# A gated mix of a long convolution and a two-layer network: the first loads in another order, and the front's constants set anew

## The chip, the cores and the metric

One core of a Trainium2 chip runs the whole program. The metric is the time of one execution in microseconds (us), told by the device. PE is the matrix engine (PEld its loads of the stationary operand), DVE the vector engine, ACT the scalar engine with its function tables, POOL the general engine, and SP the engine that issues most DMAs.

## The reference, cut to what matters

```python
g = sigmoid((x * gate_w).sum(-1, keepdims=True))           # x: 1 x 2048 x 512
a = conv_s4(x, ...)                                        # K[d, l] from exp(dt * A * l), FFT convolution, + x * Dskip
b = gelu(x @ w1 + b1) @ w2 + b2                            # 512 -> 1792 -> 512, gelu by tanh
return g * a + (1 - g) * b
# K = einsum("dn,dnl,dn->dl", C, exp(dt * A * l), dt * B).real, l = 0 .. 2047, n = 0 .. 127, dt = exp(log_dt)
```

## The kernel before

Everything is fp32. The network's matmuls are made of three: each operand is split into a high part (`xh`, `wh`, `hh`: a cast to the type fp32r, on ACT or DVE) and a low part (`xlo`, `wl`, `hl`: a subtraction on DVE).

The program has two stages. The first, `front`, interleaves four streams. `dense` is the network: eight blocks of 256 rows of x, each with the first halves of w1 and w2 (seven tiles of 128 columns of w1, seven of 128 rows of w2), and then the eight blocks once more with the other halves. `hidden` makes h (lines 915 to 917, into the bank `ph`), gelu follows on ACT (932) with a cast (935), and `output` adds to `acc` (960 to 962). `taps` makes the convolution's kernel for four groups of 128 channels, each in four chunks: `prepare`, `coefficients`, `powers`, `magnitudes` and `rotate` on DVE and ACT (line 710 is the last product of a chunk), then `contract` on PE (724, bank `pk`), and for each two chunks `first_stage` (436, the first half of the FFT), whose result ACT copies to `sk` (750) and SP stores to `tk_d` (765). `signal` does the first half of the FFT of x (also 436) and stores it to `tu_d`; `early` loads that back (479). The second stage, `conv`, loads `tk_d` (1107), does the second half of both transforms on PE (1130), multiplies, goes back (1169, 1288), and writes the output; the network's last products (1223 to 1225) stand in it.

The order inside `front` is made by a planner while the program is built. Each piece of work is a `Task` on one engine with a length, a due time and what it reads and writes. `Plan.run` then plays the program through with a model of the engines and of the DMA wire, and takes on each engine, of the tasks that are ready, the one that is due first (line 262). The due times come from the block of constants at the top of the file (`T_0` to `N_G`). The engines' queues on the chip are those orders; an engine does its queue strictly one after another.

At the head, `dense` loads block 0 of x in two halves (`load_x`, line 841, tiles of `attic`, with line 817), then the fourteen weight tiles of the first halves (line 1010; they are put into `sk` and `y`, which are free then), the biases `b2b` (b2 in all partitions, 1013) and `b1t` (1014). `first_dt` loads the first group's parameters `pr` (A, B, C in rows 0 to 5 and the logarithm of the step sizes, `dtb`, in row 6) and makes exp of row 6 by `make_dt`: four small operations on DVE, one Exp on ACT, six on DVE. `other_dts` does the same for all 512 channels in a 128 x 4 tile (`dts`). `warm` runs 13 matmuls on zeros ahead of all (1021). `W_CAST` and `X_CAST` say which of the first casts DVE does (1) and which ACT (0).

Of the kernel before, what the change touches and what calls it, by code (L numbers as in the profile page):

```python
# [30 lines left out]
CW = 32  # L31
NCH = UW // CW
NB = 2 * NSB
T_0 = 27.471
T_MLP = 406.143
K_0 = 33.386
T_KG = 350.924
U_0 = 29
U_GAP = 18
LAG = 13.052  # L40
TABLE = 29.71
D_KA = -39.892
D_KP = -35.012
D_S1 = -14.111
D_EV = -27.491
D_H = -65.233
D_LO = -24.455
PS = (2, 3, 1, 2)
N_ACC, N_H, N_PK, N_PU = PS
D_SP = 7.909  # L50
MEM = (6, 2, 3)
N_LD, N_HL, N_ST = MEM
D_XS = -121.487
D_G = 1.255
N_WARM = 13
T_EARLY, T_LOFT, T_DEN = 396.538, 396.243, 586.499
Y_K, Y_U = 42.618, 26.868
W_MLP = (-0.0424, -0.0297, 0.0179)
W_KG = (-0.036, -0.031, -0.0271)
W_U = (-0.0356, -0.1227, -0.0106)  # L60
D_MAG = -0.973
D_ROT = 0.757
D_CON = -0.676
D_PHA = 0.468
D_PRE = -2.033
D_XL = 34
D_COE = -4.518
D_OUT = -4.432
D_LAST = -43.443
N_REST = 3  # L70
D_KA0 = 31
D_DT = 0
D_PRM = -608.49
D_D0 = -398.939
D_WAVE0 = -358.845
D_COE0 = -16.66
D_SP1 = -365.247
D_G0 = 4
D_GW = 477.286
D_XS0 = 64.773  # L80
T_PRE = 2
W_CAST = (0, 0, 0, 0, 0, 0, 0, 0, 1, 1, 0, 1, 0, 0)
X_CAST = (1, 1, 1, 0)
D_X0, D_B2, D_B2A, D_DM = -479.848, -229.497, -81.364, 94.739
N_G = 6

N_ATTIC, N_LOFT, N_TK = 11, 8, 8
ASIDE = (4, 6, 13, 14)
# [110 lines left out]
SLOW = 1.18  # L199
# [23 lines left out]
class Plan:  # L223
# [26 lines left out]
    def run(self, fixed=None):  # L250
        clock = Clock()
        free = dict.fromkeys(("PE", "ACT", "DVE", "SP", "GP"), 0.75)
        ready = {p: [] for p in free}
        for t in self.tasks:
            t.left, t.ready = len(t.deps), 0.0
            if not t.left:
                ready[t.part].append(t)
        heads = {p: list(ts)[::-1] for p, ts in fixed.items()} if fixed else None
        table, order, wire, lanes, turn = None, [], 0.0, [], None

        def key(t):
            return t.due + (TABLE if t.table and t.table != table else 0.0), t.n

        for _ in self.tasks:
            best = None
            for p, ts in ready.items():
                if heads:
                    ts = [heads[p][-1]] if heads[p] and not heads[p][-1].left else ()
                if ts:
                    at = max(free[p], min(t.ready for t in ts))  # L270
                    if p == "SP" and len(lanes) >= LANES:
                        at = max(at, lanes[-LANES])
                    if best is None or at < best[0]:
                        best = at, p
            at, p = best
            if heads:
                t = heads[p].pop()
            else:
                t = min((t for t in ready[p] if t.ready <= at), key=key)
                ready[p].remove(t)  # L280
            hold = t.hold
            if p == "PE":
                hold = clock.run(at, hold + TURN_PE * (t.turn != turn), t.rows)
                turn = t.turn
            if t.table and t.table != table:
                table, hold = t.table, hold + max(1.283 - (at - free[p]), 0.0)
            free[p] = at + hold
            t.at = at
            end = at + hold + t.lat
            if t.wire:  # L290
                took, (before, behind) = t.wire
                wire = max(wire, at + before) + took * (SLOW if at > 22.0 else 1.0)
                end = wire + behind
                if p == "SP":
                    lanes.append(end)
            t.end = end
            order.append(t)
            for u in t.users:
                u.left -= 1
                u.ready = max(u.ready, free[p] if u.part == p == "PE" else end)  # L300
                if not u.left and not heads:
                    ready[u.part].append(u)
        self.end = max(t.end for t in order)
        self.order = order
        return order
# [3 lines left out]
def gated_mix(  # L309
# [18 lines left out]
    nc = tc.nc  # L328
# [22 lines left out]
    def front(pool, psum, keep, attic, loft, den):  # L351
# [18 lines left out]
        def move(kb, fn, due, reads=(), writes=(), queue="SP", out=False, hold=0.4, rate=360.0):  # L370

            before, behind = OUT if out else IN
            wire = kb / rate, ((before, behind) if queue == "SP" else (2.2, 0.75))
            return pl.add(queue, hold if queue == "SP" else hold + 0.2, fn, due, reads, writes, wire=wire)
# [16 lines left out]
        pr = pool.tile([P, 7, UW], F32, name="pr")  # L391
        dtb = pr[:, 6]
# [33 lines left out]
        def first_stage(xs, due, evac, ahead=2):  # L426
# [10 lines left out]

            mm(1.04, products, due + D_S1, [*(key for _, key in xs), "c1"], [key for _, key in banks], 0.5, 1.06, "f32")
            for r, (bank, key) in enumerate(banks):
# [4 lines left out]
        def signal():  # L444
            for s in range(8):
                t = U_0 + 16 * U_GAP * warp(s / 8, W_U)
                yield t + Y_U
# [4 lines left out]
                def evac(r, pp, key, s=s, t=t):  # L452
                    k = take("st", N_ST)
                    act(512, lambda: nc.scalar.copy(st[k], pp), t + D_EV, [key], [("st", k)])
                    for m in range(2):
# [54 lines left out]
        def first_dt():  # L510

            k, r, ki = (loft[:, 2048 + UW * m : 2048 + UW * m + UW] for m in range(3))
            move(459, lambda: nc.sync.dma_start(pr, prm[0]), D_PRM, [], ["pr", "dtb"])
            make_dt(dtb, k, r, ki.bitcast(I32), ["tt", "dtb"], D_D0, dtb)

        def other_dts():
# [30 lines left out]
        def prepare(u, t, eb_k):  # L547
            sl = slice(u * UW, (u + 1) * UW)
            eb = parts(eb_k, 6 * UW, 1)
            kx = ("xc", eb_k)  # L550
            act_due = t + D_KA + (0 if u else D_KA0)
            if u:
# [91 lines left out]
        def waves(t):  # L644
# [4 lines left out]

            act(99 * CW, sines, t + D_KA, ["ph"], ["tt"], "sin", ops=5)  # L650

        def begin(c, k, t):

            cs = slice(c * CW, (c + 1) * CW)
            act(
                8 * CW, lambda: nc.scalar.copy(xc[k][:, :, 0:4], x4[:, :, :, cs]), t + D_KA,  # L656
                ["x4"], [("xc", k)],
# [14 lines left out]
        def magnitudes(u, c, t):  # L672

            cs = slice(c * CW, (c + 1) * CW)

            pl.add("GP", 0.13, lambda: nc.gpsimd.memset(e[:, 63], 1.0), t + D_KA, [], ["y1"])
            act(CW, lambda: nc.scalar.copy(e[:, 0], ea[u % 2][:, 5, cs]), t + D_KA, [("ea", u % 2)], ["y1"])  # L677

# [35 lines left out]
        def contract(u, c, k, t):  # L714
# [18 lines left out]
            for g0 in (0, 4):  # L733
                mm(1.89, lambda g0=g0: products(g0), t + D_KP, ["y0", "y1", ("xc", k)], [("pk", q)], lat=0.41, turn="f32")

# [4 lines left out]
            at0 = pks[q][:, 63]  # L740
            vec(8, lambda: nc.vector.tensor_add(at0, at0, d0), t + D_LO, ["dm"], [("pk", q)])
            act(512, lambda: nc.scalar.copy(xs, pks[q].rearrange("p s g -> p (s g)")), t + D_S1, [("pk", q)], [key])
            pair.append((xs, key))
# [3 lines left out]
            def evac(r, pp, key):  # L747
# [5 lines left out]
                    ),  # L753
                    t + D_EV, [key], [("sk", c // 2, r)],
                )
# [16 lines left out]
        def taps():  # L772
            first_dt()
            other_dts()
            nc_ = D // UW
            gap = T_KG / (nc_ * NCH)
            nth = 0
            t = K_0
            yield t
# [8 lines left out]
            for g in range(nc_ * NCH):  # L788
                u, c = divmod(g, NCH)
                k = nth % 2  # L790
                t = K_0 + T_KG * warp(g / (nc_ * NCH), W_KG)
                yield t + Y_K
# [57 lines left out]
        def split_x(b, loaded, due):  # L850
# [7 lines left out]
            for d, x, n in ((xh_d, xh, "xh"), (xl_d, xlo, "xl")):  # L858
                move(
                    512, lambda d=d, x=x: nc.sync.dma_start(d[b], x[k].bitcast(F32)), due + (D_XS if b > 1 else D_XS0),  # L860
                    [(n, k, 0), (n, k, 1)], [(n + "_d", b)], out=True,
# [14 lines left out]
        def gates(b0, b1_, t):  # L876
# [11 lines left out]
            )  # L888
            vec(220, sides, t + D_LO, [], keys)

# [14 lines left out]
        def hidden(i, t):  # L905
# [24 lines left out]
            def gelu():  # L930
# [8 lines left out]
            act(  # L939
                2 * nf * SB, gelu, t + D_H, ["b1"], [hk, ("h", q)], "gelu",  # L940
                ops=nf + 3.3,
# [4 lines left out]

            vec(nf * SB, low, t + D_LO, [hk, ("h", q)], [lk])

        def output(i, t):
# [16 lines left out]
            for s in range(2):  # L966
                if b == NB - 1 or i == 4 * NB - 6:
# [5 lines left out]
                    0.2295 * 3 * len(fs), lambda s=s, q=q: products(s, acc[q]),  # L973
                    t + LAG + D_OUT * (j == 3) + D_LAST * (b == NB - 2) * j,
                    [hk, lk, *ws], [("acc", q)], lat=0.45,
                )
                if j == 3:
# [3 lines left out]
                        512, lambda q=q, r=r: nc.scalar.copy(io[r], acc[q]),  # L981
                        t + D_EV, [("acc", q)], [("io", r)],
                    )
# [16 lines left out]
        def dense():  # L1000
# [46 lines left out]
            for i in range(4 * NB):  # L1047
                t = T_0 + T_MLP * warp(i / (4 * NB), W_MLP)
                yield t
# [10 lines left out]
                if j == 1 and b + 1 < NSB:  # L1060
                    split_x(b + 1, x, t + (D_SP if b else D_SP1))
                if 27 <= i < 29:
# [4 lines left out]
                if 29 <= i <= 32:  # L1067
                    for r in range(2):
                        for f in cols(i + 3):
                            split_w(f, r, *raw[f, r], t + D_SP)  # L1070
                            fetch(t)
# [318 lines left out]
```

## Time and profile before

| | |
|---|---|
| three runs | median 509.49 us (508.29 to 511.25) |
| the profiled execution | 509.49 us, span of its instructions 507.7 us, mean granted clock 0.993 |
| busy share of the span | PE 98%, DVE 84%, ACT 69%, POOL 11% |
| DMA | 112.3 MB, 221 GB/s in the mean |

The span runs from the first to the last instruction; the other 1.8 us lie around it. PE's share is high throughout, so what is left to see lies at its edges: before its first useful matmul, in the stretch at a lowered clock, in waits between it and the engines that feed it, and behind its last matmul.

### The profile page before, as it was taken

The numbers are of one execution on the slowest core, as the hardware profiler recorded it, in microseconds if no ns is written. First come the engines' busy times: TensorE is split into PE (matmuls) and PEld (weight loads), VectorE is DVE, ScalarE is ACT, GpSimd is POOL, SyncE is SP. The second block draws the span as 40 slices with busy tenths as digits, with TensorE's granted clock in tenths as the row PEclk, the third lists the DMA queues.
The fourth block names the chain that finished last, engine by engine and source line by source line (L and its number), as shares of the span: only waits on it lengthen the run. The fifth ranks groups of instructions, "written<-read, shape, count | busy, mean of one in ns | idle before, by whom it ended". The sixth has DMA issues, their size and how long they took to land.

```text
span 507.7 us, 12168 instructions
## 1 busy us (share of the span) xinstructions
PE 496.2 (98%) x4794; PEld 379.8 (75%) x4794; DVE 427.7 (84%) x789; ACT 349.7 (69%) x629; POOL 53.6 (11%) x92
## 2 busy tenths in 40 slices
PE   6999999999999999999999999999999999999996
PEld 5998878888789888889889888978889722222451
DVE  4999999999999999999999999799921288877544
ACT  3999746698793789985769998456642545558513
POOL 1001010101001102012001010101010300120003
PEclk8899999999999999999999999999999999999999
DMA  7967995546889432989733366883479998999997
GB/s 261 377 233 215 321 293 166 106 151 162 213 226 314 76 125 96 251 201 208 172 107 43 117 134 161 202 302 65 130 256 192 261 358 301 345 372 383 311 337 303
DMA packets 82391, 112.30 MB, mean 221 GB/s; under 512 B 39612, under 2 KB 40768, under 8 KB 81792
## 3 DMA queue, kind: packets, MB, share of 16 engines
q1 hardware_dynamic: 74144, 86.41, 53.1%
q0 software_dynamic: 7264, 21.73, 18.2%
q10 hardware_dynamic: 928, 3.41, 1.9%
q8 instruction: 37, 0.61, 0.5%
q14 instruction: 18, 0.15, 0.1%
HBM read 61.71 MB, written 49.81 MB: 220 GB/s over the span
## 4 chain that ended last, share of the span: by engine, by line
PE 69%; DVE 14%; ACT 8%; DMA 4%; issue 3%; SPq 1%; DVEq 0%; ACTq 0%
PE pk L724 9%; PE ph L915 7%; PE ph L917 6%; PE ph L916 6%; PE acc L960 6%; PE acc L962 6%; PE p2u L1130 6%; PE acc L961 6%; PE p2k L1130 5%; PE pa L1169 3%; PE pb L1288 3%; DMA sk<-in_w_dram 2%; DVE y L687 2%; PE ph L436 2%; DVE loft L531 2%
## 5 line engine op out<-in xcount | busy, mean ns | idle before, releaser
L915 PE MATMUL ph<-xh,wh 128*128 128x256 f32 x448 | 129.3, 289 | 3.8 <-ACT wh L824 3.8
L917 PE MATMUL ph<-xh,wl 128*128 128x256 f32 x448 | 128.0, 286 | 0.2 <-DVE wl L826 0.2
L916 PE MATMUL ph<-xlo,wh 128*128 128x256 f32 x448 | 127.8, 285 | 0.0
L915 PEld LDWEIGHTS ph<-xh,wh 128*128 128x128 f32 x448 | 86.3, 193 | 12.6 <-issue 6.8
L916 PEld LDWEIGHTS ph<-xlo,wh 128*128 128x128 f32 x448 | 86.4, 193 | 1.7
L917 PEld LDWEIGHTS ph<-xh,wl 128*128 128x128 f32 x448 | 86.2, 192 | 0.5 <-DVE wl L826 0.5
L960 PE MATMUL acc<-wh,hh 128*128 128x512 f32 x206 | 82.9, 402 | 0.0
L932 ACT ACTIVATE ph<-ph,b1t 128x256 f32<-128x256 f32 x112 | 50.5, 451 | 46.8 <-PE ph L917 45.0
L962 PE MATMUL acc<-wh,hl 128*128 128x512 f32 x206 | 80.8, 392 | 0.9 <-DVE hl L945 0.9
L961 PE MATMUL acc<-wl,hh 128*128 128x512 f32 x206 | 81.0, 393 | 0.0
L724 PE MATMUL pk<-y,den 128*32 128x64 f32 x2048 | 61.8, 290 | 0.5 <-DVE y L710 0.4
L724 PEld LDWEIGHTS pk<-y,den 128*32 128x32 f32 x2048 | 57.2, 136 | 5.2 <-issue 3.7
L945 DVE TENSOR_TENSOR hl<-ph,hh 128x512 fp32r<-128x512 f32 (+1 forms) x62 | 38.4, 620 | 21.1 <-ACT hh L935 20.6
L960 PEld LDWEIGHTS acc<-wh,hh 128*128 128x128 f32 x206 | 38.7, 188 | 15.5 <-issue 6.0
L687 DVE TENSOR_TENSOR y<-y,ea 128x64 f32<-128x64 f32 (+4 forms) x80 | 45.5, 569 | 4.6 <-ACT y L677 4.4
L962 PEld LDWEIGHTS acc<-wh,hl 128*128 128x128 f32 x206 | 38.7, 188 | 10.9 <-DVE hl L945 2.4
L961 PEld LDWEIGHTS acc<-wl,hh 128*128 128x128 f32 x206 | 38.7, 188 | 5.9
L935 ACT CAST hh<-ph 128x512 fp32r<-128x512 f32 (+1 forms) x62 | 33.1, 533 | 9.1 <-PE acc L961 7.4
L530 DVE TENSOR_TENSOR loft<-den,zz 128x256 f32<-128x256 f32 (+2 forms) x48 | 37.4, 780 | 1.7 <-ACT den L656 1.2
L531 DVE TENSOR_TENSOR loft<-den,zz 128x256 f32<-128x256 f32 (+2 forms) x48 | 37.3, 777 | 0.0
L699 DVE TENSOR_TENSOR y<-y,loft 128x2048 f32<-128x2048 f32 x16 | 36.6, 2288 | 0.1
L1138 ACT COPY k<-p2k 128x512 f32<-128x512 f32 x32 | 18.6, 585 | 22.3 <-PE p2k L1130 8.6
(186 smaller groups left out, 871.6 us busy)
## 6 DMA issues: line engine op xcount, KB each, us to landing
tu_d<-attic SPq DMA_DIRECT2D x64, 128.0 KB, 3.7
tk_d<-sk SPq DMA_DIRECT2D x32, 256.0 KB, 5.2
t_d<-sa SPq DMA_DIRECT2D x32, 256.0 KB, 4.6
tk<-tk_d SPq DMA_DIRECT2D x24, 256.0 KB, 5.1
attic<-in_xt_dram SPq DMA_DIRECT2D x16, 256.0 KB, 5.7
xh_d<-xh SPq DMA_DIRECT2D x8, 512.0 KB, 4.7
xl_d<-xlo SPq DMA_DIRECT2D x8, 512.0 KB, 5.1
attic<-in_xs_dram SPq DMA_DIRECT2D x16, 256.0 KB, 4.9
```

Of the source, the lines that this page charges most:

```text
L531: vec(2 * m, lambda: vv.tensor_mul(v, a, bi), due, [ka, *kb], [kv])
L687: nc.vector.tensor_mul(both(n, 64 - 3 * n, n), both(0, 64 - n, n), an)
L724: nc.tensor.matmul(pks[q][32 * j : 32 * j + 32, :, gg], x[:, r, :, ch], y[:, r, :, ch], start=(r == 0), stop=(r == 1), skip_group_check=True,)
L915: nc.tensor.matmul(p, h, xh[xk][:, d], start=(d == 0), stop=False)
L916: nc.tensor.matmul(p, h, xlo[xk][:, d], start=False, stop=False)
L917: nc.tensor.matmul(p, lo, xh[xk][:, d], start=False, stop=(d == 3))
L932: nc.scalar.activation(phs[q][:, n], phs[q][:, n], AF.Gelu_apprx_tanh, bias=b1t[:, f : f + 1])
L945: nc.vector.tensor_sub(lo, phs[q][:, 0:nf], hi.bitcast(F32))
L960: nc.tensor.matmul(a, h, wh[1][w], start=start, stop=False)
L961: nc.tensor.matmul(a, h, wl[1][w], start=False, stop=False)
L962: nc.tensor.matmul(a, l, wh[1][w], start=False, stop=(j == 3))
L1130: nc.tensor.matmul(out[64 * i : 64 * i + 64], w, x, start=True, stop=True)
```

## The change

Two rules of the planner's wire model, one load, and nearly all constants of `front` are changed. `conv` is as it was.

```diff
@@ Plan.run
-        table, order, wire, lanes, turn = None, [], 0.0, [], None
+        table, order, wire, lanes, turn = None, [], 2.8, [], None
...
-                wire = max(wire, at + before) + took * (SLOW if at > 22.0 else 1.0)
+                wire = max(wire, at + before) + took * (SLOW if at > 22.0 else 1.6 if 3.2 < at < 4.2 else 1.15)
@@ first_dt
-            move(459, lambda: nc.sync.dma_start(pr, prm[0]), D_PRM, [], ["pr", "dtb"])
+            move(90, lambda: nc.sync.dma_start(dtb, prm[0, :, 6]), D_DTB, [], ["dtb"])
+            move(393, lambda: nc.sync.dma_start(pr[:, 0:6], prm[0, :, 0:6]), D_PRM, [], ["pr"])
@@ constants (three of some sixty)
-W_CAST = (0, 0, 0, 0, 0, 0, 0, 0, 1, 1, 0, 1, 0, 0)
-X_CAST = (1, 1, 1, 0)
-D_X0, D_B2, D_B2A, D_DM = -479.848, -229.497, -81.364, 94.739
+W_CAST = (0, 0, 0, 0, 0, 0, 1, 0, 1, 1, 0, 1, 0, 0)
+X_CAST = (1, 0, 1, 1)
+D_X0, D_B2, D_B2A, D_DM = -480, 22, -6.941, -38.906
```

Lines behind the new ones carry numbers that are 1 or 2 higher than before. The built programs show what that does. On SP the program begins so before (`pr` the parameters, `attic` x, `sk` and `y` the weights):

```order
L513 DMA pr<-in_prm_dram 128x896
L817 DMA attic<-in_xt_dram 128x512 x2
L1013 DMA b2b<-in_b_dram 128x512
L1010 DMA sk<-in_w_dram 128x512 x2
L1014 DMA b1t<-in_b_dram 128x14
L1010 DMA sk<-in_w_dram 128x512 x5
L1010 DMA y<-in_w_dram 128x512
L1010 DMA sk<-in_w_dram 128x512
L1010 DMA y<-in_w_dram 128x512 x5
```

And so now:

```order
L819 DMA attic<-in_xt_dram 128x512 x2
L514 DMA pr<-in_prm_dram 128x128
L1012 DMA sk<-in_w_dram 128x512 x2
L1016 DMA b1t<-in_b_dram 128x14
L1012 DMA sk<-in_w_dram 128x512 x5
L1012 DMA y<-in_w_dram 128x512
L1012 DMA sk<-in_w_dram 128x512
L515 DMA pr<-in_prm_dram 128x768
L1012 DMA y<-in_w_dram 128x512 x5
```

x is first, the step sizes alone are second (64 KB), the other parameters (384 KB) stand behind nine weights, and `b2b` is gone from here; it comes behind all weights and the first two loads of the signal. The stores of `xh` and `xlo`, which followed the weights, now come behind six loads more.

On DVE the head before is this (491 to 494 and 499 to 504 are `make_dt`, 822 and 826 casts and subtractions):

```order
L494 SCALAR_TENSOR_TENSOR loft<-loft 128x128
L822 CAST xh_105<-attic 128x512 x2
L499 TENSOR_TENSOR loft<-loft 128x128
L500 TENSOR_TENSOR loft<-loft 128x128
L501 TENSOR_SCALAR loft<-loft 128x128
L502 TENSOR_SCALAR loft<-loft 128x128
L503 CAST loft<-loft 128x128
L504 TENSOR_TENSOR pr<-loft 128x128
L826 TENSOR_TENSOR xlo_107<-attic,xh_105 128x512 x2
L826 TENSOR_TENSOR wl_123<-sk,wh_109 128x512
L826 TENSOR_TENSOR wl_124<-sk,wh_110 128x512
```

And now, from the last of the four small operations on:

```order
L495 SCALAR_TENSOR_TENSOR loft<-loft 128x128
L828 TENSOR_TENSOR xlo_107<-attic,xh_105 128x512
L828 TENSOR_TENSOR wl_123<-sk,wh_109 128x512
L500 TENSOR_TENSOR loft<-loft 128x128
L501 TENSOR_TENSOR loft<-loft 128x128
L502 TENSOR_SCALAR loft<-loft 128x128
L503 TENSOR_SCALAR loft<-loft 128x128
L504 CAST loft<-loft 128x128
L505 TENSOR_TENSOR pr<-loft 128x128
L828 TENSOR_TENSOR wl_124<-sk,wh_110 128x512
```

The six later operations moved from ahead of all weights to between the first and the second. One half of block 0 of x is cast on ACT now, both halves of block 1 on DVE, and one more weight.

At the end of `front`, on ACT, this stands around the copies of the last first stage (`s` its input, `sk` its result, `io` a finished block of the network) before:

```order
L742 COPY s_104<-pk_90 128x512
L981 COPY io_143<-acc_85 128x512
L981 COPY io_144<-acc_86 128x512
L750 COPY sk<-ph_88 128x64x8
L750 COPY sk<-pk_90 128x64x8
L750 COPY sk<-pu_91 128x64x8
L750 COPY sk<-pu_92 128x64x8
L932 ACTIVATE ph_87<-ph_87,b1t 128x256 x2
L935 CAST hh_138<-ph_87 128x512
```

And now:

```order
L983 COPY io_143<-acc_85 128x512
L744 COPY s_104<-pk_90 128x512
L983 COPY io_144<-acc_86 128x512
L934 ACTIVATE ph_87<-ph_87,b1t 128x256 x2
L937 CAST hh_138<-ph_87 128x512
L752 COPY sk<-ph_88 128x64x8
L752 COPY sk<-pk_90 128x64x8
L752 COPY sk<-pu_91 128x64x8
L752 COPY sk<-pu_92 128x64x8
```

A gelu pair and its cast moved ahead of the four copies. On PE the last first stage stands at row 1926 of 2335 before and at row 1950 now: twenty-four matmuls of `hidden` moved ahead of it. On SP the eight stores to `tk_d` at this place are followed by two loads of `tu_d` before:

```order
L479 DMA loft<-tu_d 128x512
L765 DMA tk_d<-sk 64x16x64 x8
L479 DMA den<-tu_d 128x512 x2
L1099 DMA cc_4756<-in_c_dram 128x384
L1107 DMA tk_4758<-tk_d 128x512
```

And by three now:

```order
L480 DMA den<-tu_d 128x512
L767 DMA tk_d<-sk 64x16x64 x8
L480 DMA loft<-tu_d 128x512
L480 DMA den<-tu_d 128x512 x2
L1101 DMA cc_4757<-in_c_dram 128x384
L1109 DMA tk_4759<-tk_d 128x512
```

One load of `tu_d` moved from ahead of the stores to behind them. Over the whole program ACT holds 44 loads of a function table, where it held 42.

More of the change, by code (lines that the diff above doesn't have):

```diff
@@ L33 @@
 NB = 2 * NSB
[L34 to L38, printed above, removed]
-U_GAP = 18
[L40 to L47, printed above, removed]
+T_0 = 28.054
+T_MLP = 403.179
+K_0 = 34.529
+T_KG = 345.899
+U_0 = 25
+U_GAP = 18
+LAG = 13.13
+TABLE = 38.817
+D_KA = -38.921
+D_KP = -51.708
+D_S1 = -41.89
+D_EV = -27.676
+D_H = -42.384
+D_LO = -24.038
 PS = (2, 3, 1, 2)
 N_ACC, N_H, N_PK, N_PU = PS
-D_SP = 7.909
+D_SP = 9.388
 MEM = (6, 2, 3)
 N_LD, N_HL, N_ST = MEM
-D_XS = -121.487
-D_G = 1.255
+D_XS = -135.205
+D_G = 2.921
 N_WARM = 13
[L56 to L69, printed above, removed]
-N_REST = 3
[L71 to L81, printed above, removed]
-W_CAST = (0, 0, 0, 0, 0, 0, 0, 0, 1, 1, 0, 1, 0, 0)
-X_CAST = (1, 1, 1, 0)
-D_X0, D_B2, D_B2A, D_DM = -479.848, -229.497, -81.364, 94.739
-N_G = 6
+T_EARLY, T_LOFT, T_DEN = 438.459, 503.927, 580.026
+Y_K, Y_U = 43.108, 32.905
+W_MLP = (-0.0418, -0.0295, 0.0149)
+W_KG = (-0.0362, -0.0266, -0.0229)
+W_U = (-0.025, -0.1293, -0.0177)
+D_MAG = -0.34
+D_ROT = 0.722
+D_CON = -1.157
+D_PHA = 0.354
+D_PRE = -1.739
+D_XL = 37
+D_COE = -4.408
+D_OUT = -1.849
+D_DTB = -224.281
+D_LAST = -4.489
+N_REST = 3
+D_KA0 = 32
+D_DT = 1
+D_PRM = -94
+D_D0 = 7
+D_WAVE0 = -296.601
+D_COE0 = -142.132
+D_SP1 = -296.865
+D_G0 = 10
+D_GW = 400.475
+D_XS0 = 271.75
+T_PRE = 12
+W_CAST = (0, 0, 0, 0, 0, 0, 1, 0, 1, 1, 0, 1, 0, 0)
+X_CAST = (1, 0, 1, 1)
+D_X0, D_B2, D_B2A, D_DM = -480, 22, -6.941, -38.906
+N_G = 7
 N_ATTIC, N_LOFT, N_TK = 11, 8, 8
```

## The prediction

> **What bounds the kernel now.** I read the page first: busy shares and the chain that ended last.
>
> ```profile
> span 507.7 us, 12168 instructions
> PE 496.2 (98%) x4794; PEld 379.8 (75%) x4794; DVE 427.7 (84%) x789; ACT 349.7 (69%) x629; POOL 53.6 (11%) x92
> PE 69%; DVE 14%; ACT 8%; DMA 4%; issue 3%; SPq 1%; DVEq 0%; ACTq 0%
> ```
>
> PE is the bound, and both orders hold the same matmuls, so the time can only move through PE's gaps, its clock, and what makes it wait. The second view sums stretches (start:end, length, busy time of PE, PEld, DVE, ACT, POOL, then granted clock, DMA share, GB/s).
>
> ```profile
> 6.60:10.35 3.75, 0.00 (x1) 0.01 (x1) 2.73 (x9) 0.62 (x1) 0.86 (x2) 0.89 0.97 299
> 10.35:16.36 6.01, 5.81 (x25) 5.51 (x26) 5.84 (x11) 4.84 (x8) 0.00 (x0) 0.50 1.02 368
> 29.00:378.40 349.40, 347.82 (x3986) 299.64 (x3984) 330.78 (x615) 264.82 (x465) 35.49 (x62) 1.00 0.66 180
> 378.40:402.60 24.20, 24.20 (x174) 22.84 (x174) 3.19 (x5) 11.05 (x23) 4.78 (x8) 1.00 0.92 218
> ```
>
> PE loses 10.35 us before its first useful matmul, then about 3 us in 6 us at clock 0.50. From 29 to 378.4 us it idles 1.6 us only, with DVE busy for 330.8 of 349.4 us beside it. The third view is the timeline of the head, with one piece of the chain (the weight issued at 3.08 lands 7.27 us later).
>
> ```profile
> 0.74 0.40 SPq L513 DMA_DIRECT2D pr<-in_prm_dram  x1
> 1.20 0.90 SPq L817 DMA_DIRECT2D attic<-in_xt_dram  x2
> 2.13 0.43 SPq L1013 DMA_DIRECT2D b2b<-in_b_dram  x1
> 2.61 0.91 SPq L1010 DMA_DIRECT2D sk<-in_w_dram  x2
> 0.99 5.60 PE L1021 MATMUL pk<-dm 128*128 128x128 f32 x26 [0.99 <-POOL dm L1016]
> 4.24 0.23 DVE L491 TENSOR_SCALAR loft<-pr 128x128 f32<-128x128 f32 x1 [3.37 <-DMA pr<-in_prm_dram]
> 7.48 0.50 DVE L822 CAST xh<-attic 128x512 fp32r<-128x512 f32 x1 [1.76 <-DMA attic<-in_xt_dram]
> 9.68 2.05 ACT L824 CAST wh<-sk 128x512 fp32r<-128x512 f32 x3 [3.95 <-DMA sk<-in_w_dram]
> 10.35 0.58 PE L915 MATMUL ph<-xh,wh 128*128 128x256 f32 x1 [3.75 <-ACT wh L824]
> 3.08 7.27 DMA sk<-in_w_dram
> ```
>
> So 448 KB had landed at 4.24, 960 KB at 7.48 and 1472 KB (with the first weight) at 9.68; PE follows 0.67 us later, after the cast.
>
> **The change, part by part.** *Start of PE.* Ahead of and with the first weight now stand x (512 KB), the step sizes (64 KB) and the weight (256 KB): 832 KB. On the line between 448 KB at 4.24 and 960 KB at 7.48 that lands at 6.7. Bounds: its issue, some 2.1, plus the quickest of the first loads (4.24 - 0.74 = 3.5) gives 5.6; plus the 7.27 of the piece above, 9.4. By bytes it is nearest to the line, so 6.7, and 6.7 + 0.7 = 7.4 for PE's first matmul, 2.95 us earlier. By the same line the second weight (1088 KB) lands at 8.0, the fourth at 10.0, and the rest 0.7 us or a little less apart (256 KB at the 368 GB/s of the second view): the seventh at 12.0.
>
> *The feeders.* PE cannot keep running from there at will: each weight is cast on ACT or DVE and subtracted on DVE, and the ten exponent operations that stood ahead of all weights on DVE are now split, six of them behind the first weight. What PE needs next and cannot run ahead of is the second block of x, and its split stands behind ACT's exponentials. The rows of that passage before:
>
> ```profile
> 16.40 1.28 ACT L932 ACT_TABLE_LOAD   x1
> 17.69 0.93 ACT L932 ACTIVATE ph<-ph,b1t 128x256 f32<-128x256 f32 x2
> 18.65 0.59 ACT L935 CAST hh<-ph 128x512 fp32r<-128x512 f32 x1
> 23.04 0.20 ACT L507 ACTIVATE dts<-dts 128x4 f32<-128x4 f32 x1
> 23.15 1.50 ACT L572 ACTIVATE loft<-pr 128x128 f32<-128x128 f32 x7
> 24.55 1.30 ACT L579 ACTIVATE ea<-pr 128x128 f32<-128x128 f32 x6
> 25.76 1.10 ACT L579 ACTIVATE den<-pr 128x128 f32<-128x128 f32 x5
> 23.28 0.16 DVE L499 TENSOR_TENSOR dts<-dts 128x4 f32<-128x4 f32 x1 [0.27 <-ACT dts L507]
> 27.56 0.69 DVE L826 TENSOR_TENSOR xlo<-attic,xh 128x512 fp32r<-128x512 f32 x1
> 28.97 0.28 PE L915 MATMUL ph<-xh,wh 128*128 128x256 f32 x1
> 29.09 0.28 PE L916 MATMUL ph<-xlo,wh 128*128 128x256 f32 x1
> ```
>
> In the new order ACT has, behind the seventh weight's cast (12.0 + 0.6 = 12.6): a table load 1.28, two gelu pairs with their casts (2 x 1.52), four weight casts (4 x 0.59), the seven scalings 1.50, a table load 1.28, the eleven exponentials 2.40 and the small one 0.20: 12.1 by durations, about 11.5 by the distance of starts in these rows; so 24.1. DVE then has six 4-column operations (1.0), two casts of x (0.8) and the two subtractions (0.6 and 0.69): one half ready at 26.5, both at 27.2, where before both were ready at 28.25. PE's own work up to there would be done at about 25 (28.97 less 2.95 and part of the slow stretch), so DVE decides: block 1 starts at about 26.6, against 28.97. The lead is **2.4 us**; bounds 0.7 (weight at 9.4) and 3.5 (weight at 5.6).
>
> The row of clock 0.50 is the place for a rule. The Trainium skill, "TensorE: Matmul & The Clock Gate", Part 1, says that a free-running window of some 3.4 us without activity halves the clock and a busy one restores it. The gap of 3.75 us and the slow 6.0 us behind it agree. By that rule the new gap, 0.8 us, would leave the clock up, and the sum at PE alone would be 2.95 + 3.0 instead of 2.4; the rows of DVE and ACT say it is not reached (rival C).
>
> *Does the lead last?* DVE runs within a microsecond of PE:
>
> ```profile
> 81.53 1.15 DVE y L710
> 82.81 3.61 PE pk L724 x120
> 369.79 1.22 DVE L710 TENSOR_TENSOR y<-y,loft 128x1024 f32<-128x1024 f32 x1
> 371.99 3.76 PE pk L724 x120
> ```
>
> At the second tap group PE waits for DVE's last product (82.68). The new order puts 2.6 us less DVE work ahead of it (counted by these rows' prices) and 1.4 us less PE work; with DVE 1.2 us early, DVE is 3.8 and PE 3.8 us early: no new wait, no slack either. At the last group there is 1.0 us of slack, and PE has 2.1 us more work ahead of it. I let the lead stand at 2.4, with 1 us on either side for waits that come or go in the middle (ACT holds two more table loads, 2 x 1.28).
>
> *The hand-over to the second stage.* The last first-stage product is row 1926 of PE's 2335 before, row 1950 now: 24 matmuls at 0.12 (29.09 - 28.97) that covered its way out are moved ahead, 2.9 us.
>
> ```profile
> 378.32 0.39 PE L915 MATMUL ph<-xh,wh 128*128 128x256 f32 x1
> 380.50 10.86 SPq L765 DMA_DIRECT2D tk_d<-sk  x8
> 391.47 2.33 SPq L479 DMA_DIRECT2D den<-tu_d  x2
> 395.14 0.79 SPq L1107 DMA_DIRECT2D tk<-tk_d  x2
> DMA to landing us min/median/max: 4.2/4.5/4.7
> DMA to landing us min/median/max: 4.2/6.8/9.5
> 402.60 0.65 PE L1130 MATMUL p2k<-tk,cc 128*64 128x512 f32 x2
> ```
>
> The first two tap loads (first landing row; the second is for the first six) land at 399.4 and 400.2; PE wants the second with its second matmul, some 0.4 us into the last row, at 403.0, so 2.8 us are spare. The change takes 2.9; a gelu and a cast (1.5) now stand ahead of ACT's four copies, 0.45 of which the 1.04 us first stage does not hide; and a third load of u stands behind the stores, 0.65. The wait is 2.9 + 0.45 + 0.65 - 2.8 = 1.2. Two accumulating DMAs of POOL also move some 3 us towards these loads: 0 to 1.3 more. I take **1.5**; bounds 0 (the stores shorten with fewer bytes beside them) and 2.5.
>
> *The rest.* The bias row and the two stores of x move behind other loads on SP; the bias serves POOL's accumulations alone, which wait for other things:
>
> ```profile
> POOL out_dram L990 <- DMA out_dram<-io: 53.6, 6, 15.1
> ```
>
> Cost nothing; without that cover POOL would be late, which PE does not see. The parameters (384 KB) stand behind nine weights: 12.0 + 1.3 + 1.0 = 14.3. DVE comes to them behind the first weight's cast (7.3), six exponent operations (6 x 0.25), eight subtractions (8 x 0.6) and two casts (0.8), at 14.4: free, but only just; if they land later, DVE loses the difference.
>
> Sum: -2.4 + 1.5 = -0.9 us. The profiled execution took 509.49 (span 507.7 and 1.8 around it), which is also the median: **508.6 us**.
>
> **Rivals.** B: the lead is kept, since the stores and loads of the hand-over fit after all. For it: 2.8 us are spare today. Against: the 2.9 us taken from it. 509.49 - 2.4, with half a microsecond of a mid stall gone: 506.6.
> C: the clock never drops and the feeders are in time. PE then gains the 2.95 and half of the 6.0 us at clock 0.50: 5.95, so 503.5. For it: the gap shrinks below the slow stretch's trigger. Against: DVE's rows above. It is what the rule of the Trainium skill named above would bring about.
> D, slower: the two tap loads are caught behind POOL's accumulations and take what the slowest of the first six took, 9.5 us instead of 4.7. The wait is then 1.2 + 4.8 = 6.0, the time 509.49 - 2.4 + 6.0 = 513.1. It decides from a landing of about 6 us on. Against: those six were issued one behind another.
> E: the change doesn't do what it says: the first weight lands no earlier since the first transfers are slow whatever their order (the second half of x, issued by about 1.7, was there at 7.48, 5.8 us later). No lead, and the hand-over's 1.5: 511.0.
>
> **How the numbers follow.** Chances: forecast 0.50, B 0.22, C 0.06, D 0.12, E 0.10. About 0.5% (2.5 us) is what a measurement of this kernel tells from no change. B lies at that edge and counts for the greater part as faster: 0.26 with C and a little of the forecast's edge; D is slower, 0.12; the rest, 0.62, is the same. The range leaves out C and D: from 505.8 (B with the earliest weight) to 511.2 (E).
>
> **What would show it.** Right: first useful matmul near 7.4 and clock 1.00 from there; a PE gap before block 1 at 25 to 27 us; block 1 at 26.6; a gap of 1 to 2 us at the first product of the second stage, ended by a load of taps. Wrong: a first matmul after 9; no gap at the second stage (B); clock 0.50 after 9.5; PE waits in the middle of more than 2 us in sum.

## The result and the profile after

The changed kernel took 515.97 us in the median (513.03 to 519.34), the kernel before 509.49: a ratio of 1.013, with a 95% interval of 1.0081 to 1.0178. On another chip the same pair gave 517.93 and 508.42, 1.0149 (1.0104 to 1.0194). One further run of the kernel before, of 775.82 us, was a slow one and is left out. The change makes the kernel slower, by 6.5 us here and 9.5 there by the medians, or 6.6 and 7.6 by the ratios, which are not those of the medians; the forecast was 508.6, with 511.2 as its upper end.

The page of the changed kernel has this (its profiled execution took 513.03 us):

```profile
span 511.0 us, 12187 instructions
PE 495.6 (97%) x4794; PEld 379.1 (74%) x4794; DVE 427.7 (84%) x790; ACT 351.5 (69%) x630; POOL 53.4 (10%) x92
PE 74%; ACT 9%; DVE 6%; DMA 6%; SPq 3%; issue 2%; DVEq 0%
```

Against before (69, 14, 8 and 4% for PE, DVE, ACT and DMA) the chain that ended last runs less over DVE and more over PE, DMA and SP. Where time is lost is seen in stretches (start:end, length, busy time of PE, PEld, DVE, ACT, POOL, then granted clock, DMA share, GB/s):

```profile
5.59:6.33 0.74, 0.38 (x5) 0.19 (x3) 0.70 (x3) 0.67 (x2) 0.00 (x0) 1.00 1.20 290
6.33:25.90 19.57, 17.02 (x110) 14.84 (x110) 18.42 (x46) 16.80 (x41) 0.71 (x2) 1.00 0.98 356
25.90:248.76 222.86, 221.34 (x2405) 191.65 (x2405) 212.38 (x412) 172.85 (x306) 21.58 (x36) 1.00 0.70 194
248.76:252.20 3.44, 0.00 (x1) 0.01 (x1) 2.72 (x8) 3.33 (x6) 0.00 (x0) 1.00 0.00 0
252.20:403.30 151.10, 151.08 (x1752) 131.63 (x1752) 119.71 (x206) 101.63 (x179) 16.77 (x28) 1.00 0.64 161
403.30:414.72 11.42, 9.77 (x41) 4.13 (x41) 6.96 (x12) 3.80 (x8) 2.49 (x4) 1.00 1.02 350
```

The head is what was hoped for and more: PE starts at 6.33 instead of 10.35, and the clock stays at 1.00. Then two places give it back: a hole of 3.44 us in the middle, with DMA idle as well, and the hand-over to the second stage, which takes 11.42 us from the front's last product to the first `pa` (before: from 402.67 to 411.34, 8.67). From the first `pa` to PE's last product it is 91.42 us in both traces.

The head and the start of block 1, from the timeline of after:

```profile
5.66 0.62 ACT L826 CAST wh<-sk 128x512 fp32r<-128x512 f32 x1 [0.40 <-DMA sk<-in_w_dram]
6.33 0.39 PE L917 MATMUL ph<-xh,wh 128*128 128x256 f32 x1 [0.36 <-ACT wh L826]
24.95 0.38 PE L917 MATMUL ph<-xh,wh 128*128 128x256 f32 x1 [0.32 <-DVE xh L824]
25.88 0.39 PE L918 MATMUL ph<-xlo,wh 128*128 128x256 f32 x1 [0.55 <-DVE xlo L828]
```

Block 1 starts at 24.95 and, after a short wait, has its second product at 25.88, which before ran at 29.09: a lead of some 3.2 us.

**The hole at 248.8.** The chain of waits and the engines' timelines there (a load, the product with the gate's weights in line 872, ACT's copy, the gate's tanh with a table load on either side, the gelu, and the first half of the signal's FFT):

```profile
222.68 11.40 SPq L767 DMA_DIRECT2D tk_d<-sk  x8
234.19 11.01 DMA attic<-in_xs_dram
245.21 0.69 DVE L872 SCALAR_TENSOR_TENSOR attic<-attic 128x512 f32<-128x512 f32 x1 [4.56 <-DMA attic<-in_xs_dram]
246.03 0.59 ACT L744 COPY s<-pk 128x512 f32<-128x512 f32 x1 [4.62 <-DVE pk L743]
247.05 1.28 ACT L888 ACT_TABLE_LOAD   x1
248.34 0.21 ACT L888 ACTIVATE gate<-gs 128x16 f32<-128x16 f32 x1
248.57 1.28 ACT L934 ACT_TABLE_LOAD   x1
251.45 0.69 DVE L947 TENSOR_TENSOR hl<-ph,hh 128x512 fp32r<-128x512 f32 x1 [0.69 <-ACT hh L937]
252.20 0.64 PE L437 MATMUL ph<-attic,c1t 32*64 32x512 f32 x1 [3.44 <-DVE hl L947]
```

The load of x rows 15 is issued behind the eight stores of `tk_d` and lands 11.01 us later. It is not alone on the wire: POOL issues two loads of 512 KB at 232.50 and 233.05, and from 234.2 to 245.2 POOL's queue takes 59.9% of the DMA engines' time and SP's 28.0%. The last of the eight stores takes 11.8 us to land, where their median is 5.3. DVE stands still for 4.56 us before the product that reads it, ACT for 4.62 behind DVE, and PE for 3.44 behind both. In the kernel before, the sixteen products of this kind were over by 124 us, when no such stores ran; `D_G` (1.255, now 2.921) spreads them. One row each of before and after, with the first and last start:

```profile
L870 DVE SCALAR_TENSOR_TENSOR attic<-attic x16: 686/692/701, 28.4 to 123.8; 128x512 f32<-128x512 f32 x16
L872 DVE SCALAR_TENSOR_TENSOR attic<-attic x16: 681/683/694, 30.5 to 245.2; 128x512 f32<-128x512 f32 x16
```

The other waits of PE in the middle are small (0.34 and 0.86 that begin at 44.3 and 45.4, ended by ACT's and DVE's work on a gelu, 0.32 at 207).

Theory T was therefore: the head's lead is real, and two places lose more than it brings, the late gate and the hand-over. Its rivals: the head's lead cannot last whatever the rest does (E); the hand-over is the whole loss (H); the granted clock is (K).

### The profile page after: what moved, and what is told of

Same layout as the page of the kernel before. It is cut to its first block, busy times and chain, and to the rows that moved or that the text cites. A ratio compares the mean times of both kernels' runs of the same rounds, so it can differ in the third digit from the quotient of the medians.

```text
span 511.0 us, 12187 instructions
## 1 busy us (share of the span) xinstructions
PE 495.6 (97%) x4794; PEld 379.1 (74%) x4794; DVE 427.7 (84%) x790; ACT 351.5 (69%) x630; POOL 53.4 (10%) x92
## 3 DMA queue, kind: packets, MB, share of 16 engines
q10 hardware_dynamic: 928, 3.41, 1.8%
## 4 chain that ended last, share of the span: by engine, by line
PE 74%; ACT 9%; DVE 6%; DMA 6%; SPq 3%; issue 2%; DVEq 0%
PE pk L726 10%; PE ph L917 7%; PE acc L962 7%; PE ph L918 7%; PE ph L919 7%; PE acc L964 6%; PE acc L963 6%; PE p2u L1132 6%; PE p2k L1132 5%; PE pa L1171 3%; PE pb L1290 3%; PE ph L437 3%; DMA attic<-in_xs_dram 2%; SPq L767 2%; DMA tk<-tk_d 2%
## 5 line engine op out<-in xcount | busy, mean ns | idle before, releaser
L917 PE MATMUL ph<-xh,wh 128*128 128x256 f32 x448 | 127.9, 285 | 0.7 <-ACT wh L826 0.4
L917 PEld LDWEIGHTS ph<-xh,wh 128*128 128x128 f32 x448 | 85.1, 190 | 7.4 <-issue 4.2
L918 PEld LDWEIGHTS ph<-xlo,wh 128*128 128x128 f32 x448 | 85.1, 190 | 2.7 <-DVE xlo L828 0.7
```

What stands on the lines that cost most here:

```text
L917: nc.tensor.matmul(p, h, xh[xk][:, d], start=(d == 0), stop=False)
L918: nc.tensor.matmul(p, h, xlo[xk][:, d], start=False, stop=False)
```

## The experiments

In all of them the planner's finished list is taken and a few tasks are moved in it (`shift(order, what, to)` puts them behind a task, or ahead of it); every engine's order is otherwise that of the kernel named. The ratios are to the kernel before, on the same chip.

### The changed kernel again (a0)

> The changed kernel once more, unaltered. All theories: 511 to 519 us, the median 1.0 to 1.8% over the kernel before. T (the time is lost at the wait of 3.44 us at 248.8, where the last product with the gate's weights waits for a load of x that sits behind eight stores): the wait is there again, between 2 and 5 us long, and where a profile shows a time near 516, a stretch at a granted clock of 0.5 stands behind it or at another gap over 3 us. K (the clock alone): the profile differs from the first one in a stretch at half clock and in nothing else.

517.93 us, 1.0149. The wait at 248.9 is 4.33 us in this profile, and a stretch at clock 0.50 stands behind it. Windows of 3.41 us, cut where the clock changes, first of a0 and then of the first profile of the changed kernel:

```profile
246.40:249.82 3.42, 2.46 (x21) 2.25 (x19) 3.42 (x10) 2.77 (x6) 0.00 (x0) 1.00 0.00 0
249.82:253.23 3.41, 0.05 (x7) 0.05 (x7) 2.68 (x8) 3.30 (x6) 0.00 (x0) 1.00 0.00 0
253.23:256.64 3.41, 3.41 (x20) 1.51 (x21) 3.41 (x5) 2.02 (x5) 0.00 (x0) 0.50 0.04 10
```

```profile
247.16:250.57 3.41, 1.60 (x14) 1.39 (x12) 3.38 (x8) 3.34 (x5) 0.00 (x0) 1.00 0.00 0
250.57:253.99 3.42, 1.79 (x19) 0.89 (x20) 2.73 (x5) 2.85 (x7) 0.00 (x0) 1.00 0.00 0
```

In a0 the hole fills one window, and the next runs at half clock; in the first profile nearly the same hole falls across two windows, PE is busy for about half of each, and the clock stays. The one profile took 516.68 us, the other 513.03. The slow stretch accounts for some 1.7 us of that (an estimate, half of 3.41); a0's longer hole and two later waits on DVE that the first profile has not (1.16 at 340.8, 0.72 at 346.3) add to it. Over the ten runs of the changed kernel on record, the time goes with the mean granted clock: 513.03 us at 0.999, and 517.94 to 519.34 in the three at 0.988 and 0.989. The clock alone (K) is not the loss: in the first profile it stays at 1.00 up to PE's last product, and the time is 3.5 us over before all the same.

### The last product and the gate 60 places later (e1)

```diff
-        for t in pl.run():
+        order = pl.run()
+        late_ones = [dot of x rows 15, the gate's tanh, its two scalings]
+        dve = [t for t in order if t.part == "DVE"]
+        order = shift(order, late_ones, dve[dve.index(dot of x rows 15) + 60])
+        for t in order:
```

> The changed kernel with the last of the gate's products (x rows 15), the tanh and its two scalings taken 60 places back in DVE's order, behind the load's landing. T: the wait of 3.44 us at the signal's first half goes down to under 0.5, the time comes 3 to 4 us below the changed kernel's of the same chip in a like run, and by its median more, 4 to 6 us (where the clock fell behind the wait): near 510, the spread of its runs under 2 us. K: the wait goes and the median moves by no more than the wait, 3.4 us, with the spread as wide as before. Rival H (the new hand-over to the second stage is the loss): no gain over 1 us, since the wait lies where PE makes it up later.

511.28 us (509.14 to 513.5), 1.0033 (1.0005 to 1.0062): under the changed kernel on the same chip by 6.6 us by the medians and 5.9 by the ratios, where T had 4 to 6. The hole is gone, and H falls: a wait in the middle counts. That the gain is more than the wait of 3.44 to 4.33 us holds for the values themselves; by their intervals it could be as little as the wait. The spread stayed wider than expected, 4.4 us.

### Only the load moved (e6 and e6b)

```diff
+        load = the load of x rows 15
+        order = shift(order, [load], last task that reads its buffer)
+        order = shift(order, [the eight stores of tk_d], load)
```

e6 put the load ahead of the first store and so, in program order, ahead of that last reading too: one weight's low part is made of rows of x there, and its time holds for the engines' orders alone. e6b has the lines above. The engines' orders are the same in both.

> The changed kernel with one DMA moved: the load of x rows 15 ahead of the eight stores instead of behind them; the gate's product, tanh and scalings stay where they are. T1 (the load's place on SP is what holds the product, DVE, ACT and PE): it is issued near 228 (its buffer comes free then) and lands by 234, so the product's wait of 4.56 us goes and PE's wait of 3.44 to 4.33 falls to under 1 us: 511 to 513, ratio to before 1.003 to 1.008. T2 (the gate's own place and its two table loads, 2.56 us, are the cause): PE still waits over 2 us and the time falls by under 2 us, ratio over 1.011. Against both: the stores come up to 6 us later, and what they hold up may wait.

> The load of x rows 15 ahead of the eight stores on SP once more, this time behind the last reading of the weights that its buffer holds before (in e6 it overtook that reading, so that one weight's low part was made of rows of x, and PE waited 1.24 us there). T1 (the load's place on SP holds DVE, ACT and PE): issued near 228, landed by 234, no wait of the gate's product over 0.5 us, PE's wait at the signal's first half under 1 us: 510.5 to 513, ratio to before 1.004 to 1.008, as e6 had 1.007. T2 (the gate's place with its two table loads): a wait of 2 us or more stays, ratio over 1.011.

e6: 511.84 us, 1.0069 (1.0041 to 1.0097). e6b: 510.37 us, 1.0023 (0.9996 to 1.0051). The two loads of x at that place in after and in e6b (first and last issue; then for these and two more, issue to landing):

```profile
L819 SPq DMA_DIRECT2D attic<-in_xs_dram x2: 328/940/1553, 222.3 to 234.2; - x2
DMA to landing us min/median/max: 4.3/5.5/11.0
```

```profile
L822 SPq DMA_DIRECT2D attic<-in_xs_dram x2: 328/328/328, 222.1 to 225.3; - x2
DMA to landing us min/median/max: 3.1/4.3/5.1
```

Issued at 225.3 instead of 234.2, the load lands in time (no more than 5.1 us later), and PE's hole goes, though the gate and both of its table loads stay where they were. T1 holds, with a gain a little over its own range, and T2 falls: the place of one DMA on SP was worth some 1.2% of the time (1.0149 to 1.0023, two chips, each against the kernel before; 0.7 to 1.8% with the noise of both). At its new place the load is ahead of the stores and of POOL's two loads at once, so these runs do not part what each of them costs it. The Trainium skill, "DMA: Bandwidth & Descriptors", section "Queues, rings and completion order", says that each DMA engine consumes the descriptors of one row in order; the 11.0 us behind eight stores and the 5.1 at most ahead of them agree, with POOL's loads as a second cause that was not tested apart.

### The old hand-over (e4), and both (e5)

```diff
+        order = shift(order, [the 24 products of hidden], the last first stage)
+        order = shift(order, [their gelu, its low part], the last of ACT's four copies)
+        order = shift(order, [the third load of u], the first store of tk_d, False)
```

> The changed kernel with the hand-over of the kernel before: the 24 products of `hidden` behind the last first-stage product again, its gelu and cast behind ACT's four copies, the third load of u behind the eight stores. Accounts of the traces so far: from the end of the front to the first product `pa` PE takes 8.73 us before and 11.4, 11.48 and 10.35 in the three kernels that have the new hand-over, 1.6 to 2.75 more, of which only 0.6 to 1.66 is seen as idle; the rest is taken by pairs of products on the two halves of the matrix engine that start 0.36 us apart where they started 0.01 apart. Theory T: all of it goes, 2 to 2.7 us under the changed kernel (ratio to before 1.010 where that had 1.015), the group p2k<-tk busy for 12.4 and 12.3 us instead of 15.0 and 14.7. Rival G (only the idle time counts, pairs out of step cost nothing): 0.6 to 1.65 us.

> Both edits: the last of the gate's products 60 places later and the old hand-over. T (the two losses stand apart and add up): 511.3 less 2.0 to 2.7 = 508.6 to 509.3, a ratio to before of 0.998 to 1.001; in the profile the front ends 2 us before that of the kernel before (near 400.5) and the end of PE's work is 2 us earlier too. Rival S (the gain of one is lost at the other, since stores and loads of the hand-over collide with what e1 moved): not under 510.5.

e4: 514.53 us, 1.0117 (1.0089 to 1.0144). e5: 508.13 us, 0.9985 (0.9962 to 1.0009). The first products of the second stage, in after and then in e4, and the group's row in each (busy, mean ns of one, idle before):

```profile
404.28 1.04 PE L1132 MATMUL p2k<-tk,cc 128*64 128x512 f32 x2 [0.98 <-ACT hh L937]
405.99 0.64 PE L1132 MATMUL p2k<-tk,cc 128*64 128x512 f32 x1 [0.67 <-DMA tk<-tk_d]
406.09 0.61 PE L1132 MATMUL p2k<-tk,f 128*64 128x512 f32 x1
...
L1132 PE MATMUL p2k<-tk,cc 128*64 128x512 f32 x48 | 15.0, 594 | 1.6 <-ACT hh L937 1.0 <-DMA tk<-tk_d 0.7
```

```profile
403.96 1.08 PE L1152 MATMUL p2k<-tk,cc 128*64 128x512 f32 x4
...
L1152 PE MATMUL p2k<-tk,cc 128*64 128x512 f32 x48 | 12.4, 594 | 0.0
```

In e4 two products on the two halves of the matrix engine start side by side; in after the second load of taps is late, the pairs begin out of step and stay so. The stage takes 8.66 us in e4 and e5, 11.42 in after: 2.75 lost, of which 1.65 is idle time. That G is wrong is shown by the two traces, in which the pairs out of step take 1.1 us beside the idle time. By the ratios the hand-over is worth 0.3% (after to e4, whose intervals overlap) to 0.5% (e1 to e5), 1.6 to 2.4 us, and the lower of these would fit G too. The two losses add up; S falls. With both taken out, e5 can't be told from the kernel before.

### Work in the hole (e7)

```diff
+            for _ in range(15):
+                nc.tensor.matmul(pus[1][:, :P], dm, dm, start=True, stop=True)
             # and then the signal's first half, the one that waits at 248.8
```

> The changed kernel with 15 more products of zeros (128x128, into a bank that the following first stage writes over) ahead of the product that waits at 248.8, some 3.2 us of PE work in the wait. It adds work to PE and takes no wait away. T with the clock (the wait, where it is over 3.4 us, also halves the granted clock for one or two stretches of 3.4 us, as in the second profile of the changed kernel): the clock stays at 1.00 behind it, and the time falls by 1 to 3 us, ratio to before 1.008 to 1.012, the spread narrower. Rival K0 (the clock has nothing to do with the wait): no gain, ratio 1.015, or a little more where the zeros outlast the wait.

515.61 us, 1.0126 (1.0086 to 1.0165). The zeros cover 3.51 us, 0.92 of the wait is left, and the clock of the profile is 1.00 throughout:

```profile
248.00 3.51 PE L1104 MATMUL pu<-dm 128*128 128x128 f32 x30
252.43 0.64 PE L437 MATMUL ph<-attic,c1t 32*64 32x512 f32 x1 [0.92 <-DVE hl L953]
```

The clock stays up in all six runs (0.995 to 1.000 in the mean, where the changed kernel had 0.988 to 0.999). The time goes in the expected direction, but the interval overlaps that of the changed kernel: by time the clock's share is not settled. By the length of the wait, 3.44 to 4.33 us, more than half of what e1 wins is the wait itself.

### The head alone (e2, e3), and its order on DVE (e9, e10)

```diff
 e2: the kernel before, with
+        order = shift(order, [x0, x1], dtb, False)            # loads: x first, the step sizes alone
+        order = shift(order, [pr], the ninth weight)
+        order = shift(order, [sub0, four], cast0); order = shift(order, [exp], wh0); order = shift(order, [six], wl0)
+        order = shift(order, [b2b], the first load of ux)     # and the two stores of x behind six loads more
 e3: the changed kernel, with the converse
 e9: e2, and
+        order = shift(order, [low part of the first gelu], the four operations on dts, False)
 e10: e9, and
+        order = shift(order, [wl0], low part of x's second half, False)
```

> The kernel before with the changed kernel's first loads alone (x, step sizes, weights, other parameters behind the ninth weight, bias behind the first loads of the signal, the two stores of x further back; DVE's first operations to match), the order of PE and POOL and everything behind the head as before. T: the lead of the head, 2.5 to 4 us, lasts to the end, since the constants and not the loads lost it: 505.5 to 507.5, faster than before by 0.4 to 0.8%. Rival E (the lead is lost at DVE, which is as late as before at the second group of taps, whatever the head does): 508.5 to 509.5, with new waits of 2 to 4 us in the middle. Rival K (a clock that falls at the head in some runs): a spread of 3 us or more.

> The changed kernel with the first loads of the kernel before (all parameters, x, bias, weights; DVE's first operations to match). T: the head's lead goes (first useful matmul near 10 us, a stretch at half clock behind it), the wait at 248 shrinks or stays, as the load's time follows SP's stores, so 1 to 4 us over the changed kernel: 514 to 517 where that has 513. Rival E (the lead is used up before 250 anyway, by DVE): the same as the changed kernel within 1 us.

> The kernel of e2 (the kernel before with the new first loads alone) with one subtraction on DVE moved: the low part of the first gelu's result ahead of four 4-column operations and two subtractions of weights instead of behind them. T (the new head's lead of 3.5 us was lost in e2 at DVE, whose order was made for weights that land later: 1.12 us at 7.4, 2.23 at 18.5): the wait of 2.23 goes down to 0.3, and 1.5 to 2 us of it last to the end: 506.5 to 507.2, ratio to before 0.994 to 0.997. Rival E (the lead is used up in the middle whatever the head does): 508 to 508.7, with longer waits at 80, 200 or 330 than the 0.17, 0.17 and 1.35 of e2.

> The kernel of e9 with one more subtraction on DVE moved: the low part of the first weight ahead of the low part of x's second half. In e9 PE waits 1.28 us at 7.5 for it, and the window of 3.41 us of the granted clock in which that lies (6.30 to 9.71, PE busy for 2.07) is followed by one at 0.50, which costs some 1.0 to 1.7 us. T (waits at the head count twice where the clock falls behind them): the wait shrinks to 0.3 to 0.6 us and the clock stays at 1.00 behind the head: 505.3 to 506.4, ratio to before 0.992 to 0.995. Rival W (the wait alone counts): 506.3 to 506.7, 0.995. Rival E (it is given back at the next wait of the head, for the second weight's or x's low part): 507, as e9.

e2: 508.66 us, 0.998 (0.9945 to 1.0014). e3: 520.04 us, 1.0202 (1.0157 to 1.0248). In e3 the first useful product is at 10.60, and the clock is at 0.50 for 6.8 us behind the head, for 6.8 us behind the hole (3.88 us at 252.7) and for 3.4 us at the hand-over. So the new head is worth some 0.5% in the changed kernel (1.0202 to 1.0149; the two intervals overlap) and, put into the old order, nothing that can be told from no change: e2 by itself came out at rival E's time. The waits of PE show why, of e2 and then of e9 (total, times, longest):

```profile
PE acc L968 <- DVE hl L951: 3.6, 2, 2.2
PE ph L923 <- DVE wl L830: 1.6, 2, 1.1
```

```profile
PE ph L923 <- DVE wl L830: 1.3, 1, 1.3
PE acc L968 <- DVE hl L951: 0.6, 2, 0.3
```

The order on DVE had been made for weights that land later. With one subtraction moved (e9) the time is 507.17 us, 0.9963 (0.9948 to 0.9978): faster than before, and the lowest ratio of all. The wait behind `hl` shrinks in the trace; by time alone e9 is not told from e2, whose interval holds all of e9's. E falls: the front ends at 399.97 there against 402.67, so 2.7 us of a lead of 3.6 (6.74 against 10.35) last to the end. e10 is a miss: 507.3 us, 0.9984 (0.9958 to 1.0009), as rival E had it. Its wait at 7.8 is 0.22 and the clock stays at 1.00 behind the head, but 1.02 stands at 9.7 for the second weight's low part, and 0.89 at 29.5.

### One gelu earlier (e8)

```diff
+        order = shift(order, [gelu 5], ACT's first copy of acc, False)
+        order = shift(order, [its low part], two products of the next parameters, False)
```

> The kernel of e5 with the gelu of the sixth set of products ahead of ACT's two copies of acc instead of behind them, and its low part ahead of two products of the next parameters on DVE. T: the waits of 0.35 at 44.0 and 0.87 at 45.0 go and nothing comes in their place: 506.9 (508.1 less 1.2), ratio to before 0.996, the end of PE's work near 499.5. Rival E (DVE is as late as before at the second group of taps, so the lead is given back there): a wait of 0.5 to 1.2 us at 83 or 207 instead, 508.

510.36 us, 1.0023 (1.0005 to 1.0041): by the ratios 2 us over e5, not under it. The two small waits are replaced by a larger one, which begins at 41.4:

```profile
PE acc L967 <- ACT io L988: 2.6, 1, 2.6
```

The copies that the gelu now passes free the banks of `acc`, and PE's next products write into these. The neighbour that was overtaken was itself awaited. The window of 3.41 us behind this wait (43.5 to 46.9) also runs at clock 0.50.

## Why the prediction was wrong, point by point

- **Start of PE**: the way right, the size short. The first weight landed at 5.63, the lower bound of 5.6 and not the 6.7 of the line by bytes: x, the step sizes and the first three weights landed 2.8 to 3.7 us after their issue, the next weights took 5.3 and more. First useful product 6.33 for 7.4. (By the line itself the second weight would have come at 8.3, not 8.0; and the lower bound of the lead, 0.7, does not follow from a weight at 9.4, which is 2.7 us behind 6.7.)
- **The feeders**: waits there as named (0.32 and 0.55 ahead of block 1, ended by DVE), but block 1 at 24.95 to 25.9 for 26.6; the lead 3.2 for 2.4, within the bounds of 0.7 to 3.5. The clock did what rival C said, and stayed up.
- **"Does the lead last?"** is the step that failed. I read it at two places of PE against DVE (the second and the last group of taps) and put all else into "1 us on either side for waits that come or go in the middle". The order on the engines showed that the gate's last product and its tanh had moved from 124 us to the middle of the front. What that product reads, where its load stands on SP and what stands ahead of it I did not follow. The measured size is 3.44 to 4.33 us of wait, 5.9 us by the ratios with what follows it (a0 to e1). It is the prediction's own sign of being wrong, "PE waits in the middle of more than 2 us in sum".
- **The hand-over**: mechanism right (the tap loads are late), term 1.5 with an upper bound of 2.5, measured 2.75 in the trace and 1.6 to 2.4 by the ratios. What was missing was the pairs out of step; the idle time alone, 1.65, fits the term. The first two tap loads took 6.4 and 7.8 us to land, where before they took 4.2 and 4.7, so the landing from which rival D was to decide was there too, with a far smaller wait than D's 6.0. The profile puts 0.98 of the idle time to ACT's last cast, which ends at 404.20; the first of the loads lands at 404.2 as well, so this trace does not say which of them held PE. In e1 it is the loads alone (1.36 and 0.30).
- **The rest**: no wait of PE ends on the bias, the stores of x or the parameters, as said. The parameters landed at 13.66 for 14.3, and DVE came to them at 14.28.
- **Rivals**: D (slower, 513.1) came nearest to the time, but by luck, since the cause was another: a load caught behind SP's stores and POOL's loads, but at 234 instead of at the hand-over. The mechanism was named, at the wrong place, with 0.12. (The ends of the range stand 0.2 to 0.3 us off the sums they name: B with the earliest weight comes to 505.5, not 505.8, and E to 511.0, not 511.2.)

The account by ratios, each with a noise of about half a percent: the head -0.5%, the late load +1.2%, the hand-over +0.3 to +0.5%; together +1.0 to +1.2% of the 1.3 to 1.5% measured. The rest, 0.1 to 0.5% or some 0.5 to 2.5 us, is not settled; the two waits at 44 and 45 are 1.2 us of it in the traces, but e8 did not free them.

## What to carry to other kernels

When a scheduler's constants change, list for each operation that crossed a large distance what it reads, and look at the queue of that load at its new place: one DMA behind eight stores held three engines here. A lead won at the head needs a feeders' order that is made for it: with one subtraction moved (e2 to e9) the waits shrank, and 2.7 us of the lead lasted. Before a task is moved ahead of a neighbour, ask who waits for the neighbour (e8).

## What the runs showed of the hardware

The clock did not need a wait as long as its window to fall. A window of 3.41 us in which PE was busy for 1.25 us was followed by one at 0.50, at the hand-over of e6b (the same view as above):

```profile
400.25:403.66 3.41, 1.25 (x6) 0.46 (x5) 1.11 (x2) 1.31 (x3) 1.25 (x2) 1.00 1.09 314
403.66:407.08 3.42, 3.08 (x9) 1.05 (x10) 0.00 (x0) 0.59 (x1) 1.23 (x2) 0.50 1.06 401
```

The wait there is 2.16 us. The Trainium skill, "TensorE: Matmul & The Clock Gate", Part 1, speaks of an idle window of some 3.4 us that runs freely; the length and the free run agree with the traces, the word idle only roughly. In the fourteen traces (before, after and the twelve experiments) cut into such windows, those at full clock with PE busy for up to 0.39 of the window were all followed by half clock, and those from 0.42 on were not, but for one at the head of e9 with 0.61, which these traces don't explain:

```profile
6.30:9.71 3.41, 2.07 (x13) 1.51 (x13) 3.27 (x10) 2.45 (x5) 0.71 (x2) 1.00 1.00 321
9.71:13.13 3.42, 3.42 (x17) 3.19 (x16) 3.39 (x7) 2.32 (x4) 0.00 (x0) 0.50 1.04 398
```

So a wait of some 2 us costs a stretch at half clock in one place and none in another, by where the window falls: the wait of 2.23 us in e2 fell across two windows, busy for 0.67 each, and the clock stayed at 1.00.
